# An MM-DiT attention block on one core: fewer changes of the TensorE tiling, text keys in four row groups, and the image gate weights moved ahead of the text V weights

## The chip, the core and the metric

The kernel runs on one core of a Trainium2 chip. The metric is the device time of one execution in microseconds (us); 8 runs of the kernel before have a median of 120.23 us, with 119.77 as the lowest and 120.82 as the highest. The tensor engine is called PE here and its weight loads PEld, the vector engine DVE, the scalar engine ACT, GpSimd POOL, and the sync engine, which only issues DMAs in this kernel, SP.

## What is computed

Two streams of tokens, image (2 batches of 256) and text (2 batches of 32), each of width D = 1152, go through one joint attention. All tensors are bf16.

```python
mod_i = (_silu(c) @ wmod_img).reshape(B, 6, 1, D)      # the same for text: mod_t
shi, sci, gai = mod_i[:, 0], mod_i[:, 1], mod_i[:, 2]  # shift, scale, gate
hi = _layernorm(x_img) * (1 + sci) + shi
qkvi = hi @ wqkv_img                                   # the same for text: qkvt
...
q = jnp.concatenate([qt, qi], axis=1)                  # k and v alike
scores = jnp.einsum('bqd,bkd->bqk', q, k) * D ** (-0.5)
p = _softmax(scores, axis=-1)
a = jnp.einsum('bqk,bkd->bqd', p, v)
at, ai = a[:, :Nt], a[:, Nt:]
out_i = x_img + gai * (ai @ wo_img)
out_t = x_txt + gat * (at @ wo_txt)
```

Of each modulation matrix only three of the six blocks of 1152 columns are used, so 14 weight blocks of 1152 x 1152 (2592 KB each) are read from memory.

## The kernel before

**Weights and their slots.** A block is held as a tile `t` of 128 partitions x 9 x 1152 in one of five slots `w0` to `w4`. SP issues the loads in the order in which they are written at the top of the kernel, and each waits for the readers of the block that held its slot. After the early loads the order is: image shift (slot 2), image Q (3), text shift (0), image K (4), text scale (1), text Q (2), text K (3), text V (1), image gate (0), text gate (2), image output (3), text output (1). So text V waits until text scale has been used on PE, and image gate waits until DVE has read the text shift weights for the last time.

**Order on PE.** The matmuls are pinned to program order (`mm` on line 61, `tr` for transposes on line 64), so PE runs exactly the written sequence: image modulation and V, then `qk_img` for Q and for K (9 groups of 9 matmuls of 512 columns each), then text Q and K (`qk_txt`), scores, text V, attention, output. Between the groups of `qk_img` hooks run small pieces of the text path: `txt_ln`, the text shift on DVE (`txt_shift_part`, accumulator `acc_sh`), `txt_transposes`, then in the K pass `txt_shift_split` (tile `hl`) and `txt_rows_scale` at group 1, `txt_rows_shift`, `txt_cols_shift` and `txt_modulate` at group 6, and `qk_txt(0)` at group 8.

**Tiling of the array.** Most matmuls use the whole 128 x 128 array. Products with few rows in the output are packed side by side in column groups: the modulation products (`mod_rows_of`, `mod_rows`, `vec_rows`) and the text scores use four groups of 32 columns (128*32 in the profile), text V and the text output two of 64 (128*64). The text keys of the attention use two row groups of 64 (64*128). The text transposes of `txt_transposes` have 64 input rows, and those of the text probabilities in `p_transposes` have 32.

**Scores and attention.** The sequence at the end of the projections is `scores_txt`, `scores_img(0)`, `img_gate`, `scores_img(1)`, `v_txt`, `p_transposes(0)`, `txt_gate`, then three `attn_pair` calls with `p_transposes(1)` after the first. Each tile of scores goes through `softmax_tile`: maximum on DVE, exponential on ACT, reciprocal and two or three multiplications on DVE into a tile `pb`. `p_transposes(b)` turns those of one batch into `pT`. The softmax output puts the 32 text keys of batch b at rows 32b of the third key block and again at 64 + 32b; the rows of the other batch are zero, from a memset of `pb` on POOL. `v_txt` likewise leaves the text values twice in `v_t`, at rows 0 and 64.

An attention tile `aps` (128 features x 288 queries of one batch) is a sum over two blocks of image keys and one of text keys. `attn_pair` has three tiles `t0` and three tiles `t1`: image keys for `t0`, then the text keys of all six tiles, then image keys for `t1`. Before, `t0` and `t1` hold six tiles in the order of batch 0, then batch 1. PSUM has six buffers for matmul results (`ps_mm`) and two for transposes (`ps_tr`).

Of the kernel before, what the change touches and what calls it, by code (L numbers as in the profile page):

```python
# [14 lines left out]
def kernel(  # L15
# [14 lines left out]
    nc = tc.nc  # L30
    bf = mybir.dt.bfloat16
# [3 lines left out]
    B, NI, D = x_img.shape  # L35
    NT = x_txt.shape[1]
    P = 128
    KT = D // P
    NTOK = NI + NT
    NIT = (B * NI) // P  # L40
    TPB = NI // P
    NTT = B * NT
# [8 lines left out]
    act = ctx.enter_context(tc.tile_pool(name="act", bufs=1))  # L51
    const = ctx.enter_context(tc.tile_pool(name="const", bufs=1))
# [3 lines left out]
    ps_tr = ctx.enter_context(tc.tile_pool(name="ps_tr", bufs=2, space=PSUM))  # L56
# [3 lines left out]
    def mm(*a, **k):  # L60
        return pin(nc.tensor.matmul(*a, **k))  # L61

    def tr(*a, **k):
        return pin(nc.tensor.transpose(*a, **k))  # L64
# [9 lines left out]
    x_t = act.tile([NTT, D], bf)  # L74
# [9 lines left out]
    def load_w(slot, src, c0, splits=(D,)):  # L84
        t = wtile(slot)
        sv = wview(src, c0)
        o = 0
        for n in splits:
            nc.sync.dma_start(t[:, :, o:o + n], sv[:, :, o:o + n])
            o += n  # L90
        return t
# [22 lines left out]
    w_k_i = load_w(4, wqkv_img, D)  # L114
    w_sc_t = load_w(1, wmod_txt, D)
    w_q_t = load_w(2, wqkv_txt, 0)
    w_k_t = load_w(3, wqkv_txt, D)
    w_v_t = load_w(1, wqkv_txt, 2 * D)
    w_ga_i = load_w(0, wmod_img, 2 * D)
    w_ga_t = load_w(2, wmod_txt, 2 * D)  # L120
    w_o_i = load_rows(3, wo_img, 0)
    w_o_t = load_rows(1, wo_txt, 0)
# [10 lines left out]
    ident = const.tile([P, P], bf)  # L133
# [14 lines left out]
        nc.gpsimd.memset(pick[:, b, b:b + 1], 1.0)  # L148
    shT32 = const.tile([P, KT, 32], bf)
    nc.gpsimd.memset(shT32[:], 0.0)  # L150

    e18 = small.tile([B * KT, P], f32, bufs=1)
    pin(nc.scalar.activation(e18[:], c18[:], ACT.Exp, scale=-1.0))
# [43 lines left out]
    def ln_rstd(var, np_, sign=1.0):  # L197
        rstd = small.tile([P, 1], f32, tag="rstd")
        pin(nc.scalar.activation(rstd[0:np_, :], var, ACT.Ln, bias=eps_t[0:np_], scale=sign))
        pin(nc.scalar.activation(rstd[0:np_, :], rstd[0:np_, :], ACT.Exp, scale=-0.5))  # L200
        return rstd

    def ln_norm(x_ap, mean, rstd, np_, out_ap):
        pin(nc.vector.tensor_scalar(out_ap, x_ap, mean, rstd[0:np_, :], op0=ALU.subtract, op1=ALU.mult))
# [120 lines left out]
    for kt in range(KT):  # L325
        for b in range(B):
            h = hT_i[:, kt, b * NI:(b + 1) * NI]
# [22 lines left out]
    def qk_img(wq, blk, hooks):  # L350
        for j in range(KT):
            for hook in hooks.get(j, ()):
                hook()
            ps = ps_mm.tile([P, B * NI], f32, tag="mm")
            for kt in range(KT):
                mm(ps[:], lhsT=wq[:, kt, j * P:(j + 1) * P], rhs=hT_i[:, kt, :],
                   start=(kt == 0), stop=(kt == KT - 1))
            qk_evac(qkT[:, blk * KT + j, :, 0:NI], ps[:].rearrange("p (b n) -> p b n", b=B), blk)
# [6 lines left out]
    v_t = act.tile([P, D], bf)  # L365
# [5 lines left out]
        nc.scalar.copy(svr[:], p_sv[:])  # L371
        cols["v"] = mod_cols_of(p_sv, "svc")

    xn_t = act.tile([NTT, D], bf)
    xT_t = act.tile([P, KT, NTT], bf)
    hT_t = act.tile([P, KT, NTT], bf)
    mod_t = const.tile([P, 2, KT, B], f32)

    def txt_ln():
        mv = ln_stats(x_t[:, :], NTT)  # L380
        ln_norm(x_t[:, :], mv[0:NTT, 0:1], ln_rstd(mv[0:NTT, 1:2], NTT), NTT, xn_t[:, :])

    def txt_transposes():
        tpt = ps_tr.tile([P, KT, NTT], bf, tag="tr")
        for kt in range(KT):
            tr(tpt[:, kt, :], xn_t[:, kt * P:(kt + 1) * P], ident[0:NTT, 0:NTT])
        nc.scalar.copy(xT_t[:], tpt[:])

    def vec_part(eng, w, acc, r0, r1, bs):
        for kt in range(r0, r1):  # L390
# [101 lines left out]
    def txt_gate():  # L492
        mod_rows(w_ga_t, 1)
        for g in range(2):
            pin(nc.gpsimd.dma_start(xf[64 * g:64 * g + NTT, :, :],
                                    xt_flat.rearrange("t (r g j) -> g t r j", r=2, g=2)[g]))
            for b in range(B):
                r0 = 64 * g + 32 * b
                nc.gpsimd.dma_start(gbf[r0:r0 + NT, :, :],
                                    gsc[1, b, :].rearrange("(r g j) -> g r j", r=2, g=2)[g].partition_broadcast(NT))  # L500
# [2 lines left out]
    shift_v_rows()  # L503
    qk_img(w_q_i, 0, {1: (txt_ln,), 2: (txt_shift_part(0, 3),), 5: (txt_shift_part(3, 6),),
                      6: (txt_transposes,), 8: (txt_shift_part(6, KT),)})
    qk_img(w_k_i, 1, {1: (txt_shift_split, txt_rows_scale,),
                      6: (txt_rows_shift, txt_cols_shift, txt_modulate),
                      8: (lambda: qk_txt(0, w_q_t),)})
    qk_txt(1, w_k_t)

# [1 line left out]
    qpos = [[0, P, 2 * P], [NT, NT + P, 0]]  # L512

    pbs = {}
    PBW = 3 * P
    pb_tiles = [act.tile([P, PBW], bf, name="pb%d" % i) for i in range(2 * B + 1)]
    for t in pb_tiles:
        nc.gpsimd.memset(t[:, NI:PBW], 0.0)

    def softmax_tile(sps, qn, key, parts):  # L520
        nmx = small.tile([P, 1], f32, tag="nmx")
        nc.vector.reduce_max(nmx[0:qn, :], sps[0:qn, :], axis=AX.X, negate=True)
        e = work.tile([P, NTOK], f32, tag="e")
        rs = small.tile([P, 1], f32, tag="rs")
        nc.scalar.activation(e[0:qn, :], sps[0:qn, :], ACT.Exp, bias=nmx[0:qn, :], scale=1.0,
                             accum_out=rs[0:qn, :])
        nc.vector.reciprocal(rs[0:qn, :], rs[0:qn, :])
        pb = pb_tiles[len(pbs)]
        nc.vector.tensor_scalar_mul(pb[0:qn, 0:NI], e[0:qn, 0:NI], rs[0:qn, :])
        for r0, r1, b in parts:  # L530
            nc.vector.tensor_scalar_mul(pb[r0:r1, NI:PBW].rearrange("p (h b n) -> p b h n", h=2, b=B)[:, b],
                                        e[r0:r1, NI:NTOK].unsqueeze(1).to_broadcast([r1 - r0, 2, NT]), rs[r0:r1, :])
        pbs[key] = pb

    def scores_img(b):
        for qi in range(TPB):
            q0 = qi * P
            sps = ps_mm.tile([P, NTOK], f32, tag="mm")
            for ft in range(KT):
                mm(sps[:], lhsT=qkT[:, ft, b, q0:q0 + P], rhs=qkT[:, KT + ft, b, :],  # L540
                   start=(ft == 0), stop=(ft == KT - 1))
            softmax_tile(sps, P, (b, qi), [(0, P, b)])

    def scores_txt():
        sps = ps_mm.tile([P, NTOK], f32, tag="mm")
        for ft in range(KT):
            for b in range(B):
                r0 = 64 * (ft % 2) + NT * b
                mm(sps[r0:r0 + NT, :], lhsT=qkT[:, ft, b, NI:NTOK], rhs=qkT[:, KT + ft, b, :],
                   start=(ft < 2), stop=(ft >= KT - 2), tile_position=(0, r0))  # L550
        half = work.tile([NTT, NTOK], f32, tag="half", bufs=1)
        nc.scalar.copy(half[:], sps[NTT:P, :])  # L552
        nc.vector.tensor_add(half[:], sps[0:NTT, :], half[:])  # L553
        softmax_tile(half, NTT, "t", [(NT * b, NT * (b + 1), b) for b in range(B)])

    pTs = {}

    def p_transposes(b):
        pT_ps = ps_tr.tile([P, 3, NTOK], bf, tag="tr")
        for qi in range(TPB):  # L560
            qp = qpos[b][qi]
            pb = pbs[(b, qi)]
            for kj in range(3):
                tr(pT_ps[:, kj, qp:qp + P], pb[:, kj * P:(kj + 1) * P], ident[:])
        qp = qpos[b][2]
        pb = pbs["t"]
        r0 = NT * b
        for kj in range(3):
            tr(pT_ps[:, kj, qp:qp + NT], pb[r0:r0 + NT, kj * P:(kj + 1) * P], ident[r0:r0 + NT, r0:r0 + NT])
        pT = work.tile([P, 3, NTOK], bf, tag="pT")  # L570
        if b == 0:
            nc.vector.tensor_copy(pT[:], pT_ps[:])
        else:
            nc.scalar.copy(pT[:], pT_ps[:])
        pTs[b] = pT

    def attn_keys(tiles, first):
# [14 lines left out]
    def attn_pair(ids0, ids1):  # L592
        t0 = {key: ps_mm.tile([P, NTOK], f32, tag="mm", name="aps") for key in ids0}
        attn_keys(t0, True)
        t1 = {key: ps_mm.tile([P, NTOK], f32, tag="mm", name="aps") for key in ids1}
        for n, key in enumerate([x for pair in zip(t0, t1) for x in pair]):
            first = key in t1
            r0, (b, dt) = 64 * (n % 2), key
            mm((t1 if first else t0)[key][:], lhsT=v_t[r0:r0 + 64, dt * P:(dt + 1) * P],
               rhs=pTs[b][r0:r0 + 64, 2, :], start=first, stop=not first, tile_position=(r0, 0))  # L600
        attn_evac(t0)
        attn_keys(t1, False)
        attn_evac(t1)

    scores_txt()
    scores_img(0)
    img_gate()
    scores_img(1)
    v_txt()
    p_transposes(0)  # L610
    txt_gate()
    G = [[(b, dt) for dt in range(d0, d0 + 3)] for b in range(B) for d0 in range(0, KT, 3)]
    attn_pair(G[0], G[1])
    p_transposes(1)
    attn_pair(G[2], G[3])
    attn_pair(G[4], G[5])

    def out_img(i, chunks, parts=None):
        b = i // TPB
# [68 lines left out]
```

## Time and profile before

| what | value |
|---|---|
| median of 8 runs | 120.23 us |
| the profiled execution: its time | 120.34 us |
| the profiled execution: its span | 118.5 us |
| PE busy | 112.9 us (95%) |
| DVE busy | 75.4 us (64%) |
| ACT busy | 41.8 us (35%) |
| POOL busy | 10.3 us (9%) |
| clock granted to PE | 1.00 |
| DMA | 40.86 MB, 345 GB/s in the mean, about 410 GB/s from 9 us to 95 us |

The span runs from the first to the last instruction of the profiled execution; its time has 1.84 us more, which lies around it. Times inside the profile count from the start of the span. The profile gives each group of instructions a start, a length and, where an engine was idle before it, the wait. The end of a matmul is modelled, so the length of a stage on PE is read from its start to the start of the next one.

### The profile page before, as it was taken

Reading aid. Unit: us, or ns where it says so; the run is one execution under the profiler, and the core shown is the slowest. Engines: PE = TensorE matmul, PEld = TensorE weight load, DVE = VectorE, ACT = ScalarE, POOL = GpSimd, SP = SyncE. Lnnn points to the kernel's source line nnn. Section 1 sums busy time; section 2 is a strip of 40 time slices with the busy share of each in tenths; the row PEclk is TensorE's granted clock in tenths of the full one; section 3 lists DMA queues with packets and bytes.
Section 4 is the critical chain, followed back from the end, with each engine's and each line's share of the span. In section 5 each row is a group of like instructions: output and inputs, shape, how many; then the busy total and the mean of one; then the engine's idle time right before and its main releaser. Section 6 shows DMA issues by size and latency. Waiting matters only on the chain.

```text
span 118.5 us, 2515 instructions
## 1 busy us (share of the span) xinstructions
PE 112.9 (95%) x1051; PEld 64.3 (54%) x1059; DVE 75.4 (64%) x157; ACT 41.8 (35%) x86; POOL 10.3 (9%) x31
## 2 busy tenths in 40 slices
PE   4998999999999999999999999999999999999990
PEld 1245544445674444445444457877876666656660
DVE  2588492062966799999999540048685666666571
ACT  5799520041752524332029232345327620000000
POOL 7120000000000000000000000000409026000000
PEclk9999999999999999999999999999999999999999
DMA  3999999999999999999999999999999997220223
GB/s 112 370 369 400 408 412 404 413 411 411 411 386 390 413 412 415 401 412 412 411 411 411 415 404 411 413 406 411 404 409 411 410 387 253 109 92 13 100 50 100
DMA packets 18613, 40.86 MB, mean 345 GB/s; under 512 B 1019, under 2 KB 1547, under 8 KB 18603
## 3 DMA queue, kind: packets, MB, share of 16 engines
q1 hardware_dynamic: 17728, 39.56, 86.0%
q0 software_dynamic: 480, 0.89, 2.3%
q10 hardware_dynamic: 395, 0.26, 0.7%
q8 instruction: 8, 0.13, 0.4%
q14 instruction: 2, 0.02, 0.0%
HBM read 39.38 MB, written 1.34 MB: 344 GB/s over the span
## 4 chain that ended last, share of the span: by engine, by line
PE 86%; DMA 8%; DVE 2%; SPq 1%; issue 1%; DVEq 0%
PE ps L61 52%; PE vps L61 15%; DMA t<-in_wmod_img_dram 8%; PE gps L61 6%; PE aps L61 6%; PE sps L61 5%; PE pT_ps L64 1%; PE sc_ps L61 1%; SPq L104 1%; DVE tmp L629 1%; DVE o L630 0%; DVE scc L217 0%; SPq L108 0%; PE tpt L64 0%; PE tp L64 0%
## 5 line engine op out<-in xcount | busy, mean ns | idle before, releaser
L61 PE MATMUL ps<-xT_i,t 128*128 128x512 bf16 x157 | 35.6, 379 | 0.3
L61 PEld LDWEIGHTS <-t 128*128 128x128 bf16 x324 | 20.4, 98 | 19.2 <-issue 0.7
L395 DVE SCALAR_TENSOR_TENSOR acc_sh<-t,sTf,acc_sh 128x1152 f32<-128x1152 bf16 x16 | 21.3, 1400 | 0.0
L61 PE MATMUL ps<-t,aT 128*128 128x384 bf16 (+3 forms) x153 | 20.2, 308 | 0.0
L61 PE MATMUL vps<-t,hS_i 128*128 128x512 bf16 (+1 forms) x106 | 17.8, 325 | 0.2
L61 PEld LDWEIGHTS <-aT 128*128 128x128 bf16 (+1 forms) x153 | 13.0, 101 | 7.1 <-issue 0.5
L61 PEld LDWEIGHTS <-hS_i 128*128 128x128 bf16 x108 | 9.0, 98 | 8.7 <-DVE hS_i L248 0.2
L629 DVE TENSOR_TENSOR tmp<-ps,gb 128x384 bf16<-128x384 f32 (+2 forms) x13 | 6.8, 527 | 6.3 <-PE ps L61 6.3
L346 ACT ACTIVATE qkT<-ps 128x512 bf16<-128x512 f32 (+2 forms) x11 | 6.2, 561 | 12.0 <-PE ps L61 12.0
L61 PE MATMUL wps<-warm 128*128 128x512 bf16 x25 | 8.6, 500 | 1.6 <-DVE unit L132 1.5
L481 POOL DMA_DIRECT2D mod_scratch<-g_sb x4 | 2.5, 636 | 76.4 <-ACT g_sb L174 76.4
L348 ACT CAST qkT<-ps 128x512 bf16<-128x512 f32 (+2 forms) x11 | 5.9, 554 | 8.2 <-PE ps L61 8.2
L172 DVE CAST v_i<-vps 128x512 bf16<-128x512 f32 x5 | 3.5, 692 | 8.2 <-PE vps L61 8.2
L553 DVE TENSOR_TENSOR half<-sps,half 64x288 f32<-64x288 f32 x1 | 0.4, 449 | 9.0 <-ACT half L552 9.0
L587 DVE TENSOR_SCALAR aT<-aps,svc 128x288 bf16<-128x288 f32 x9 | 4.5, 517 | 2.6 <-PE aps L61 2.5
L61 PEld LDWEIGHTS <-warm 128*128 128x128 bf16 x26 | 2.8, 118 | 5.8 <-issue 3.3
L61 PEld LDWEIGHTS <-sT 128*32 128x32 bf16 x180 | 4.4, 96 | 2.6 <-issue 1.8
L174 ACT CAST v_i<-vps 128x512 bf16<-128x512 f32 x4 | 2.3, 580 | 9.9 <-PE vps L61 9.9
L61 PE MATMUL sps<-qkT 128*128 128x288 bf16 (+1 forms) x54 | 5.6, 288 | 0.0
L61 PE MATMUL aps<-pT,v_i 128*128 128x288 bf16 x36 | 5.3, 287 | 0.0
L589 ACT ACTIVATE aT<-aps,svc 128x288 bf16<-128x288 f32 x9 | 4.1, 498 | 3.0 <-PE aps L61 2.9
L61 PE MATMUL gps<-t,sT 128*32 128x288 bf16 x144 | 5.1, 287 | 0.0
(104 smaller groups left out, 108.1 us busy)
## 6 DMA issues: line engine op xcount, KB each, us to landing
t<-in_wqkv_txt_dram SPq DMA_DIRECT2D x3, 2592.0 KB, 17.2
t<-in_wmod_img_dram SPq DMA_DIRECT2D x2, 2592.0 KB, 15.0
t<-in_wqkv_img_dram SPq DMA_DIRECT2D x2, 2592.0 KB, 20.4
t<-in_wmod_txt_dram SPq DMA_DIRECT2D x2, 2592.0 KB, 16.2
t<-in_wmod_txt_dram SPq DMA_DIRECT2D x3, 864.0 KB, 14.2
t<-in_wo_img_dram SPq DMA_DIRECT2D x3, 864.0 KB, 13.0
t<-in_wo_txt_dram SPq DMA_DIRECT2D x3, 864.0 KB, 12.2
t<-in_wqkv_img_dram SPq DMA_DIRECT2D x3, 576.0 KB, 10.1
```

Source lines behind the costliest of these rows:

```text
L61: return pin(nc.tensor.matmul(*a, **k))
L64: return pin(nc.tensor.transpose(*a, **k))
L104: nc.sync.dma_start(x_i[:, b * TPB:(b + 1) * TPB, :], x_img[b].rearrange("(p t) d -> p t d", t=TPB))
L172: nc.vector.tensor_copy(out_ap, in_ap)
L174: nc.scalar.copy(out_ap, in_ap)
L346: nc.scalar.mul(out_ap, in_ap, SCALE)
L348: nc.scalar.copy(out_ap, in_ap)
L395: pin(eng.scalar_tensor_tensor(acc[:, b, :], w[:, kt, :], sTf[:, kt, b:b + 1], acc[:, b, :], op0=ALU.mult, op1=ALU.add))
L481: nc.gpsimd.dma_start(gsc[si, b, :].rearrange("(g j) -> g j", g=NGG), g_sb[b:P:32, :])
L587: nc.vector.tensor_scalar(dst, tiles[(b, dt)][:], bias, None, op0=ALU.add)
L589: nc.scalar.activation(dst, tiles[(b, dt)][:], ACT.Identity, bias=bias)
L629: nc.vector.tensor_mul(tmp[:, 0:n], ps[:, 0:n], gb[:, b, c0:c0 + n])
```

## The change

- Order of loads: the image gate block is loaded before the text V block.
- `txt_ln` writes the normalized text in two halves, features 0 to 639 in rows 0 to 63 and features 640 to 1151 in rows 64 to 127; `txt_transposes` then makes five transposes of 128 x 128 in place of nine of 64 x 128, and two evictions in place of one.
- `txt_rows_scale` moves from group 1 to group 6 of the K pass, directly ahead of `txt_rows_shift`.
- `scores_img(0)` runs ahead of `scores_txt`, so that the text scores and the image gate, which have the same tiling, are neighbours.
- `p_transposes` transposes the text probabilities as whole 128 x 128 tiles. The columns written too much are overwritten by the next transpose. For batch 1 a rotated identity `ident2` brings its rows 32 to 63 to the front. `p_transposes(1)` moves from after the first `attn_pair` to directly after `p_transposes(0)`, ahead of `txt_gate`.
- An `attn_pair` now holds three tiles of batch 0 and the same three of batch 1, and its text keys use four row groups of 32 rows (rows 0, 32, 64, 96).
- The memsets of the `pb` tiles move to the start of POOL's program, together with the new memsets and the two copies that make `ident2`.

```diff
     w_k_t = load_w(3, wqkv_txt, D)
+    w_ga_i = load_w(0, wmod_img, 2 * D)
     w_v_t = load_w(1, wqkv_txt, 2 * D)
-    w_ga_i = load_w(0, wmod_img, 2 * D)
     w_ga_t = load_w(2, wmod_txt, 2 * D)
...
+    KH = (KT + 1) // 2
+    xn_t = act.tile([P, KH * P], bf)
+    nc.gpsimd.memset(pb_txt[:], 0.0)
+    nc.gpsimd.memset(xn_t[NTT:P, (KT - KH) * P:KH * P], 0.0)
+    for t in pb_tiles:
+        nc.gpsimd.memset(t[:, NI:PBW], 0.0)
+    ident2 = const.tile([P, P], bf)
+    nc.gpsimd.tensor_copy(ident2[:, 0:P - NT], ident[:, NT:P])
+    nc.gpsimd.tensor_copy(ident2[:, P - NT:P], ident[:, 0:NT])
...
-        ln_norm(x_t[:, :], mv[0:NTT, 0:1], ln_rstd(mv[0:NTT, 1:2], NTT), NTT, xn_t[:, :])
+        rstd = ln_rstd(mv[0:NTT, 1:2], NTT)
+        for h, (c0, c1) in enumerate(((0, KH * P), (KH * P, D))):
+            ln_norm(x_t[:, c0:c1], mv[0:NTT, 0:1], rstd, NTT, xn_t[NTT * h:NTT * (h + 1), 0:c1 - c0])
...
-        tpt = ps_tr.tile([P, KT, NTT], bf, tag="tr")
-        for kt in range(KT):
-            tr(tpt[:, kt, :], xn_t[:, kt * P:(kt + 1) * P], ident[0:NTT, 0:NTT])
-        nc.scalar.copy(xT_t[:], tpt[:])
+        tpt = ps_tr.tile([P, KH, 2, NTT], bf, tag="tr")
+        for k in range(KH):
+            tr(tpt[:, k].rearrange("p h t -> p (h t)"), xn_t[:, k * P:(k + 1) * P], ident[:])
+        for h, (k0, k1) in enumerate(((0, KH), (KH, KT))):
+            nc.scalar.copy(xT_t[:, k0:k1, :], tpt[:, 0:k1 - k0, h, :])
...
-    qk_img(w_k_i, 1, {1: (txt_shift_split, txt_rows_scale,),
-                      6: (txt_rows_shift, txt_cols_shift, txt_modulate),
+    qk_img(w_k_i, 1, {1: (txt_shift_split,),
+                      6: (txt_rows_scale, txt_rows_shift, txt_cols_shift, txt_modulate),
                       8: (lambda: qk_txt(0, w_q_t),)})
...
-        pT_ps = ps_tr.tile([P, 3, NTOK], bf, tag="tr")
-        for qi in range(TPB):
...
-            tr(pT_ps[:, kj, qp:qp + NT], pb[r0:r0 + NT, kj * P:(kj + 1) * P], ident[r0:r0 + NT, r0:r0 + NT])
+        pT_ps = ps_tr.tile([P, 8 * P], bf, tag="tr")
+
+        def one(kj, pb, qp, perm):
+            o = kj * NTOK + qp
+            tr(pT_ps[:, o:o + P], pb[:, kj * P:(kj + 1) * P], perm[:])
+
+        for kj in range(3):
+            if b:
+                one(kj, pbs["t"], qpos[b][2], ident2)
+            for qi in range(TPB):
+                one(kj, pbs[(b, qi)], qpos[b][qi], ident)
+            if not b:
+                one(kj, pbs["t"], qpos[b][2], ident)
...
-            r0, (b, dt) = 64 * (n % 2), key
-            mm((t1 if first else t0)[key][:], lhsT=v_t[r0:r0 + 64, dt * P:(dt + 1) * P],
-               rhs=pTs[b][r0:r0 + 64, 2, :], start=first, stop=not first, tile_position=(r0, 0))
+            first, (b, dt) = key in t1, key
+            r0 = 64 * (n // 2 % 2) + NT * b
+            mm((t1 if first else t0)[key][:], lhsT=v_t[r0:r0 + NT, dt * P:(dt + 1) * P],
+               rhs=pTs[b][r0:r0 + NT, 2, :], start=first, stop=not first, tile_position=(r0, 0))
...
+    scores_img(0)
     scores_txt()
-    scores_img(0)
     img_gate()
     scores_img(1)
     v_txt()
     p_transposes(0)
+    p_transposes(1)
     txt_gate()
-    G = [[(b, dt) for dt in range(d0, d0 + 3)] for b in range(B) for d0 in range(0, KT, 3)]
-    attn_pair(G[0], G[1])
-    p_transposes(1)
-    attn_pair(G[2], G[3])
-    attn_pair(G[4], G[5])
+    for d0 in range(0, KT, 3):
+        attn_pair(*[[(b, dt) for dt in range(d0, d0 + 3)] for b in range(B)])
```

More of the change, by code (lines that the diff above doesn't have):

```diff
@@ L150 @@
     nc.gpsimd.memset(shT32[:], 0.0)
+    PBW = 3 * P
+    pb_tiles = [act.tile([P, PBW], bf, name="pb%d" % i) for i in range(2 * B)]
+    pb_txt = act.tile([P, PBW], bf, name="pbt")
+    KH = (KT + 1) // 2
[7 more added lines that the diff above has]
+    nc.gpsimd.tensor_copy(ident2[:, P - NT:P], ident[:, 0:NT])
     e18 = small.tile([B * KT, P], f32, bufs=1)
@@ L372, in shift_v_rows @@
         cols["v"] = mod_cols_of(p_sv, "svc")
-    xn_t = act.tile([NTT, D], bf)
     xT_t = act.tile([P, KT, NTT], bf)
@@ L514 @@
     pbs = {}
[L515 to L518, printed above, removed]
     def softmax_tile(sps, qn, key, parts):
@@ L527, in softmax_tile @@
         nc.vector.reciprocal(rs[0:qn, :], rs[0:qn, :])
-        pb = pb_tiles[len(pbs)]
+        pb = pb_txt if key == "t" else pb_tiles[key[0] * TPB + key[1]]
         nc.vector.tensor_scalar_mul(pb[0:qn, 0:NI], e[0:qn, 0:NI], rs[0:qn, :])
@@ L558, in p_transposes @@
     def p_transposes(b):
-        pT_ps = ps_tr.tile([P, 3, NTOK], bf, tag="tr")
-        for qi in range(TPB):
[L561 to L567, printed above, removed]
-        for kj in range(3):
-            tr(pT_ps[:, kj, qp:qp + NT], pb[r0:r0 + NT, kj * P:(kj + 1) * P], ident[r0:r0 + NT, r0:r0 + NT])
+        pT_ps = ps_tr.tile([P, 8 * P], bf, tag="tr")
+        def one(kj, pb, qp, perm):
+            o = kj * NTOK + qp
+            tr(pT_ps[:, o:o + P], pb[:, kj * P:(kj + 1) * P], perm[:])
+        for kj in range(3):
+            if b:
[4 more added lines that the diff above has]
+                one(kj, pbs["t"], qpos[b][2], ident)
+        pT_v = pT_ps[:, 0:3 * NTOK].rearrange("p (k n) -> p k n", k=3)
         pT = work.tile([P, 3, NTOK], bf, tag="pT")
         if b == 0:
-            nc.vector.tensor_copy(pT[:], pT_ps[:])
+            nc.vector.tensor_copy(pT[:], pT_v)
         else:
-            nc.scalar.copy(pT[:], pT_ps[:])
+            nc.scalar.copy(pT[:], pT_v)
         pTs[b] = pT
@@ L596, in attn_pair @@
         for n, key in enumerate([x for pair in zip(t0, t1) for x in pair]):
-            first = key in t1
-            r0, (b, dt) = 64 * (n % 2), key
-            mm((t1 if first else t0)[key][:], lhsT=v_t[r0:r0 + 64, dt * P:(dt + 1) * P],
-               rhs=pTs[b][r0:r0 + 64, 2, :], start=first, stop=not first, tile_position=(r0, 0))
+            first, (b, dt) = key in t1, key
+            r0 = 64 * (n // 2 % 2) + NT * b
+            mm((t1 if first else t0)[key][:], lhsT=v_t[r0:r0 + NT, dt * P:(dt + 1) * P],
+               rhs=pTs[b][r0:r0 + NT, 2, :], start=first, stop=not first, tile_position=(r0, 0))
         attn_evac(t0)
```

## The prediction

> **What bounds the kernel now.** I read the page first, then PE's timeline of the second half, then the issues of the DMA queue and their landings. The page:
>
> ```profile
> PE 112.9 (95%) x1051; PEld 64.3 (54%) x1059; DVE 75.4 (64%) x157; ACT 41.8 (35%) x86; POOL 10.3 (9%) x31
> PE   4998999999999999999999999999999999999990
> DMA  3999999999999999999999999999999997220223
> PE ps L61 52%; PE vps L61 15%; DMA t<-in_wmod_img_dram 8%; PE gps L61 6%; PE aps L61 6%; PE sps L61 5%; PE pT_ps L64 1%; PE sc_ps L61 1%; SPq L104 1%; DVE tmp L629 1%; DVE o L630 0%; DVE scc L217 0%; SPq L108 0%; PE tpt L64 0%; PE tp L64 0%
> ```
>
> PE is in the chain of waits for 86% of the span, without a hole from 14.65 us to the last evictions at 114.8, at clock 1.00. So time taken out of PE's sequence comes off the end one for one, unless something else is late next. The DMA row names the candidate: it is full until 95 us, and weights don't come earlier because PE is earlier. The stages that change, in PE's timeline (start, length, tile of the array, columns, count):
>
> ```profile
> 46.60 0.43 PE L64 MATMUL tpt<-ident,xn_t 64*128 64x64 bf16 x9
> 46.97 7.94 PE L61 MATMUL ps<-xT_i,t 128*128 128x512 bf16 x35
> 54.84 1.29 PE L61 MATMUL gps<-t,sT 128*32 128x288 bf16 x36
> 56.06 9.89 PE L61 MATMUL ps<-xT_i,t 128*128 128x512 bf16 x44
> 65.88 0.67 PE L61 MATMUL gps<-hl,pick 128*32 128x288 bf16 x16
> ...
> 77.14 3.21 PE L61 MATMUL sps<-qkT 128*32 128x288 bf16 x36
> 80.28 1.29 PE L61 MATMUL gps<-t,sT 128*32 128x288 bf16 x36
> 81.50 2.38 PE L61 MATMUL sps<-qkT 128*128 128x288 bf16 x18
> ...
> 86.38 0.68 PE L64 MATMUL pT_ps<-ident,pb 128*128 128x128 bf16 x9
> 86.99 1.29 PE L61 MATMUL gps<-t,sT 128*32 128x288 bf16 x36
> 88.21 0.91 PE L61 MATMUL aps<-pT,v_i 128*128 128x288 bf16 x6
> 89.05 0.54 PE L61 MATMUL aps<-pT,v_t 64*128 64x288 bf16 x6
> 89.52 0.91 PE L61 MATMUL aps<-pT,v_i 128*128 128x288 bf16 x6
> 90.27 0.67 PE L64 MATMUL pT_ps<-ident,pb 128*128 128x128 bf16 x9
> 90.87 0.91 PE L61 MATMUL aps<-pT,v_i 128*128 128x288 bf16 x6
> 91.71 0.72 PE L61 MATMUL aps<-pT,v_t 64*128 64x288 bf16 x6
> 92.36 1.64 PE L61 MATMUL aps<-pT,v_i 128*128 128x288 bf16 x12
> ```
>
> A stage lasts from its start to the next start. See that the text keys of the middle pair take 0.65 us (91.71 to 92.36), the others 0.47.
>
> **Price of a change of tiling.** Single instructions of the trace give it. Matmuls of 512 columns start 216 ns apart; from the last of them to the first of the 36 gate products it is 309 ns. Groups of four of these start 113 ns apart; from the last one back to 512 columns it is 218 ns. So one change costs about 0.10 us (0.093 in, 0.105 out).
>
> **What the Trainium skill says.** "TensorEngine Tiling (Array Packing)", Key Properties: changing the tiling mode, not merely the tile, drains TensorE; the 0.10 us agrees. "TensorE: Matmul & The Clock Gate", Part 3: matmuls in distinct row groups start within about 4 ns of each other and run together, and four tiles of K=32 measured 3.07 times; before, pairs in two row groups start 4 ns apart and the next pair 119 to 130 ns later, but four row groups are in no row of this trace. "DMA: Bandwidth & Descriptors", Queues, rings and completion order: each DMA engine consumes a ring in order; this agrees with loads that land in the order of issue, the 16 pieces of one spread over 2.5 us.
>
> **The change, part by part.**
>
> 1. Text transposes. Before, from the regular end of the 512-column matmul (46.29 + 0.22 = 46.51) to 46.97: 0.46 us, two changes included. After, five transposes of 128 columns at 56 ns (the spacing of `pT_ps` at 86.38), no change of tiling: 0.29. **-0.17.** The norm on DVE becomes two instructions for one of 0.57; I take +0.1 us on DVE, bounds 0 and 0.4. ACT's second copy is hidden: `xT_t` is ready 20 us before its use.
> 2. `txt_rows_scale` beside `txt_rows_shift`: 36 products move, one change in and one out vanish. **-0.20.** The 16 shift products then end at 66.1 (66.48 less 0.37), so DVE's transposes and modulation, which end 3.0 us later, keep their distance of 0.9 to `qk_txt` (70.38, now 70.0). They start at 65.5, their last four at 65.9, and need `hl`, which DVE ends at 65.41; ACT now runs both `hl` copies in succession, which saves about 0.15 and pays for the norm. No wait.
> 3. `scores_img(0)` ahead of `scores_txt`. Before, four changes lie between `qk_txt` and `scores_img(1)`; two vanish (0.20). Within the text scores one group starts 211 ns after its predecessor where the rest take 112: it waits for the last eviction of `qkT` (ACT, 77.25 + 0.32). After, the image scores reach that part 0.7 us after they begin. **-0.30.** Image scores begin at 76.7, text scores at 79.0, gate at 79.6, `scores_img(1)` at 80.8, text V at 83.1.
> 4. `p_transposes`: before, 86.38 to 86.99 and 90.27 to 90.87, 1.21 in all. After, 18 transposes at 55.5 ns, 0.01 at entry and 0.10 at the exit: 1.11. **-0.10.**
> 5. Text keys in four row groups: six matmuls as four and two, so two steps of 119 ns and not three: 0.47 becomes 0.36, thrice 0.12. In the middle pair a wait of 0.18 vanishes as well (it started beside ACT's copy of `pT` of batch 1, 90.97 + 0.88; now that copy, worked out at 87.2 to 88.05 behind the evictions of `v_t`, is 0.8 ahead of its first use at 88.9). **-0.53.**
>
> Sum **-1.30 us**. Output then starts at 93.85 in place of 95.16. Evictions of an `attn_pair`, three each on ACT and DVE in 1.5 us, fit its cycle of 1.93. The last pair now evicts batch 0 features that the first output needs, by 94.1; their turn on PE is at 94.8.
>
> **What is late next.** Softmax: DVE's built order puts the text tile between the two batches. Rebuilt with the lengths of this trace (maximum 0.44, exponential to reciprocal 0.62, multiplications 0.35 and 0.25, text chain 3.4 from half copy to last multiplication) the last probabilities of batch 1 are done at 85.9; before:
>
> ```profile
> 85.86 0.25 DVE L531 TENSOR_SCALAR pb<-e,rs 128x64 bf16<-128x64 f32 x1
> ```
>
> PE now wants them at 86.3, not at 90.3 as before: 0.4 us of slack. Weights: a block takes 6.5 us of the stream. Text K lands at 66.9 (earliest pieces 64.4), then 73.4, 79.9 (now image gate, used at 80.28), then text gate, issued at 72.94:
>
> ```profile
> t<-in_wmod_txt_dram SPq DMA_DIRECT2D x1, 2592.0 KB, 13.3
> ```
>
> So it lands at 86.25, where PE wants it at 86.8 (before 86.99): 0.55 us of slack. The swap matters: with the image gate block at 79.9 and PE there at 79.6, PE would wait 0.3; now it is in place at 73.4, and text V at 79.9 is wanted at 83.1. Moved past SP's queue: the image gate waits for DVE's last read of the text shift weights at 62.6 (plus 0.1), and text V behind it for the scale products, 66.0, not 56.2. At 62.7 only text K is queued, and its first engines run dry at 64.4; the first x load, issued at 0.73 into an empty queue, landed its 576 KB by 4.3, of which transfer is about 1.5, so data flow some 2 us after issue: no gap worth a count, bounds 0 and 1.5 us. Image output weights land by 92.8, wanted from 93.85, its last third at 94.8. POOL's additions (two memsets, two copies, and the `pb` memsets, 0.79 before, moved ahead; about 1.7 us) lie in its idle 2.66 us before 5.48, and `sel` follows later; if they overran, the modulation products at 10.2 still have 4 us. The gate row on POOL starts 1.3 earlier with image gate, so its broadcast does too.
>
> The profiled execution took 120.34 us, 118.5 of span and 1.84 around it; less 1.30 it is 119.04. The median of the runs is 0.11 below it: **118.9 us**.
>
> **Rivals.**
>
> A. A wait takes the place of what is removed: probabilities or text gate weights come 0.6 to 1.3 us later than worked out. For: slacks of 0.4 and 0.55 against a sum from one execution. Against: both ends come from measured lengths. Each microsecond past the slack costs one: 119.1 to 119.8.
>
> B. Four row groups don't overlap. If only two run together, step 5 keeps 0.18: 119.3. If none do, six steps of 119 ns make 0.83 a pair, +0.36 twice and +0.18, sum +0.13 for the change: 120.4. Against: column groups of 32 do overlap in fours (113 ns a group), and pairs of row groups do.
>
> C. Slower: the weight stream runs dry at 64 to 67 us, since image gate now is issued behind text K alone and nothing is queued behind it until 66. Every later block slips by the gap. Decisive point: beyond 0.55 us the text gate at 86.8 waits one for one; the gain is gone at 1.85 and it is slower by over 0.3% from 2.2. With a gap of 3 us: 120.23 - 1.30 + 2.45 = 121.4. Against: 4.2 us lie between issue and text K's end.
>
> D. The change doesn't do what it says: the built order shows five and 18 whole transposes, both moves and the swap, so I give it nothing.
>
> **Chances.** As worked out (118.5 to 119.3): 0.76. A: 0.10. B: 0.08, half of it within 0.3% of before. C: 0.06. About 0.3% (0.36 us) is what a measurement of this kernel can tell from no change. Faster 0.88, same 0.06, slower 0.06. The range of 118.3 to 119.9 takes in A and the nearer part of B; C and the far end of B are left out.
>
> **What would show it.** Right: `tpt` x5 without a gap, 36 and 16 `gps` products adjacent, image scores starting at 76.7, 18 transposes in 1.1 us from 85.7, text keys in 0.36, output from 93.85. Wrong: PE idle before the text gate, released by DMA (C, A) or before a transpose, released by DVE (A); six text key starts 119 ns apart (B); DMA share below 9 tenths between 62 and 70 us (C).

## The result and the profile after

The changed kernel takes 118.91 us in the median, the kernel before 120.25 us in the same comparison: a ratio of 0.9888, with a 95% interval of 0.9863 to 0.9912. Slow executions at a lower granted clock are left out of every median and ratio here: one of the changed kernel (194.93 us at 0.572), and three with the old order of loads (123.72 to 124.40 us at 0.971 to 0.986). The profiled execution took 119.09 us, with a span of 117.3 us.

The page after, for the lines of the page shown of before (engines, PE's row, the rate of the DMA in GB/s, the chain of waits by engine and by line):

```profile
PE 111.0 (95%) x1047; PEld 64.0 (55%) x1055; DVE 75.5 (64%) x158; ACT 41.8 (36%) x87; POOL 11.2 (10%) x34
...
PE   4997999999999999999999999999999999999990
...
GB/s 104 386 394 401 399 410 407 411 411 413 413 396 366 409 412 411 407 410 412 411 414 384 337 406 409 414 405 410 405 411 408 410 381 413 190 99 7 101 50 101
...
PE 55%; DVE 24%; DMA 14%; issue 3%; SPq 1%; ACT 1%; DVEq 0%; ACTq 0%
PE ps L61 28%; DVE acc_sh L409 16%; PE vps L61 12%; DMA t<-in_wmod_img_dram 8%; DMA x_t<-in_x_txt_dram 6%; PE aps L61 5%; PE sps L61 4%; PE gps L61 3%; DVE hl L417 2%; DVE acc_sh L407 1%; DVE stats L194 1%; PE pT_ps L64 1%; PE sc_ps L61 1%; SPq L104 1%; DVE tmp L640 1%
```

PE is still full in nearly every slice and has lost 1.9 us of busy time. The chain has changed: 24% of it now runs over DVE, through `acc_sh` and `hl`, and 6% over the load of `x_t`. In the kernel before, no part of that path was in the chain. The DMA rate has a dip that it did not have, 384 and 337 in slices 21 and 22 (of 40, counted from 0), about 62 to 67 us. The row of the kernel before, which has 411 and 415 there:

```profile
GB/s 112 370 369 400 408 412 404 413 411 411 411 386 390 413 412 415 401 412 412 411 411 411 415 404 411 413 406 411 404 409 411 410 387 253 109 92 13 100 50 100
```

PE's timeline of the stages that changed (start, length, tile of the array, columns, count):

```profile
46.37 0.44 PE L64 MATMUL tpt<-ident,xn_t 128*128 128x128 bf16 x5
46.65 17.65 PE L61 MATMUL ps<-xT_i,t 128*128 128x512 bf16 x79
64.23 1.29 PE L61 MATMUL gps<-t,sT 128*32 128x288 bf16 x36
65.34 0.98 PE L61 MATMUL gps<-hl,pick 128*32 128x288 bf16 x16
66.25 4.06 PE L61 MATMUL ps<-xT_i,t 128*128 128x512 bf16 x17
...
76.82 3.09 PE L61 MATMUL sps<-qkT 128*128 128x288 bf16 x36
79.62 1.39 PE L61 MATMUL gps<-t,sT 128*32 128x288 bf16 x36
80.94 2.38 PE L61 MATMUL sps<-qkT 128*128 128x288 bf16 x18
...
86.39 0.28 PE L64 MATMUL pT_ps<-ident,pb 128*128 128x128 bf16 x2
...
86.72 0.28 PE L64 MATMUL pT_ps<-ident,pb 128*128 128x128 bf16 x2
86.93 1.29 PE L61 MATMUL gps<-t,sT 128*32 128x288 bf16 x36
...
88.99 0.42 PE L61 MATMUL aps<-pT,v_t 32*128 32x288 bf16 x6
89.34 1.64 PE L61 MATMUL aps<-pT,v_i 128*128 128x288 bf16 x12
...
93.94 20.17 PE L61 MATMUL ps<-t,aT 128*128 128x384 bf16 x153
```

Three things are to be seen. The text keys (`v_t`) take 0.35 us from their start to the next start, where they took 0.47 and once 0.65. The output starts at 93.94, 1.22 us earlier than before. And the 16 shift products, 65.34 to 66.25, take 0.91 us where they took 0.60 and should now take no more: single matmuls show that the last four start 418 ns after the third group, not 113. They wait for DVE:

```profile
63.30 2.66 DVE L417 TENSOR_TENSOR hl<-acc_sh,hl 128x1152 bf16<-128x1152 f32 x2
```

`hl` is ready at 65.96 and the last four products start at 66.01.

**A measure finer than the time.** One execution differs from the next mainly in when its first image V matmul starts (13.83 to 15.33 us in the profiles of this study), because that waits for the first modulation weights. From there to the first output matmul PE's sequence repeats to about 0.01 us, waits apart. I call this the stretch. Before, it is 80.51 us (14.65 to 95.16); in the profile after, 79.42 us, of which 0.31 is the wait for `hl`. What follows the stretch on PE takes 20.2 us in both kernels.

### The profile page after: what moved, and what is told of

Read it like the earlier page. It is cut to its first block, busy times and chain, and to the rows that moved or that the text cites. A ratio compares the mean times of both kernels' runs of the same rounds, so it can differ in the third digit from the quotient of the medians.

```text
span 117.3 us, 2511 instructions
## 1 busy us (share of the span) xinstructions
PE 111.0 (95%) x1047; PEld 64.0 (55%) x1055; DVE 75.5 (64%) x158; ACT 41.8 (36%) x87; POOL 11.2 (10%) x34
## 4 chain that ended last, share of the span: by engine, by line
PE 55%; DVE 24%; DMA 14%; issue 3%; SPq 1%; ACT 1%; DVEq 0%; ACTq 0%
PE ps L61 28%; DVE acc_sh L409 16%; PE vps L61 12%; DMA t<-in_wmod_img_dram 8%; DMA x_t<-in_x_txt_dram 6%; PE aps L61 5%; PE sps L61 4%; PE gps L61 3%; DVE hl L417 2%; DVE acc_sh L407 1%; DVE stats L194 1%; PE pT_ps L64 1%; PE sc_ps L61 1%; SPq L104 1%; DVE tmp L640 1%
## 5 line engine op out<-in xcount | busy, mean ns | idle before, releaser
L61 PE MATMUL ps<-t,aT 128*128 128x384 bf16 (+3 forms) x153 | 20.2, 308 | 0.0
L61 PE MATMUL wps<-warm 128*128 128x512 bf16 x25 | 7.7, 458 | 1.7 <-DVE unit L132 1.5
L532 DVE TENSOR_REDUCE nmx<-sps 128x1 f32<-128x288 f32 x4 | 1.7, 451 | 8.9 <-PE sps L61 8.9
L61 PE MATMUL ps<-hT_t,t 128*128 128x64 bf16 x162 | 5.0, 193 | 0.0
```

## Experiments

Two theories stood against each other at the start. The first: PE's sequence sets the time, each part gains what it takes out of it, and a new wait for `hl` costs 0.3 us in the changed kernel. The second: the waits that the change uncovers, of DVE or of the weights, take the place of what was removed, and a part that looks cheap holds up another.

**The control** is the changed kernel itself, unedited.

> The changed kernel itself, as a control beside its variants. Both theories: about 118.9 us. The theory that the new wait for hl on DVE belongs to the kernel expects the gap in the last four shift products of the text (tile gps from hl and pick) again, 0.2 to 0.4 us long; the rival that it was a chance of one execution expects none, with PE 0.3 us earlier from there on.

Measured: 118.94 us. Its profiled execution has no gap in the shift products:

```profile
64.66 0.66 PE L61 MATMUL gps<-hl,pick 128*32 128x288 bf16 x16
65.25 1.04 PE L61 MATMUL ps<-xT_i,t 128*128 128x512 bf16 x3
```

The stretch is 79.11 us, 0.31 shorter than in the first profile. `hl` was ready 51.06 us after the first image V matmul; PE wanted it at 51.20, and in the first profile it came at 51.45. The difference is the load of `x_t`: DVE began its statistics 22.45 us after that matmul here and 22.83 there. So the wait is not part of every execution, and the first theory's systematic 0.3 us falls. Two more profiles with the same norm and the same late issue of `x_t`, of the old order of loads and of the row groups undone below, have no wait either (`hl` at 50.90 and 50.96). What remains is that the slack is about 0.1 us.

**The load of `x_t` earlier**, on ACT's queue:

```diff
+    pin(nc.scalar.dma_start(x_t[:], xt_flat[:, :]))
     v_open(A1, 0, 3)
...
-    pin(nc.scalar.dma_start(x_t[:], xt_flat[:, :]))
     v_open([(3, 1)], 0, KT)
```

> The changed kernel with the load of x_t issued on ACT's queue some 15 us earlier, so that the text norm on DVE need not wait for it. Theory: in the changed kernel the chain x_t load, norm, acc_sh, hl ends 0.3 us after PE wants hl; with x_t there in time DVE starts its statistics at about 35.8 instead of 37.3, hl is ready about 1.5 us earlier, the gap of 0.3 in the text shift products goes, and the image gate block is issued 1.5 us earlier, so the dip of the DMA rate at 62 to 67 us goes too. Time 0.3 us below the control. Rival: the 0.3 is taken back at the text gate, whose weights land at 86.5 where PE then comes at 86.6, or the earlier x_t delays the V weights at 15 to 20 us: same time as the control, within 0.1, with a wait released by DMA.

Measured: 118.93 us, and a stretch of 79.11. DVE starts its statistics 21.15 us after the first image V matmul and `hl` is ready at 49.72, 1.5 us before it is wanted. The time does not move, so the wait for `hl` is not worth anything that the median shows; with six and seven runs an effect of 0.3 us could hide there, and what speaks is the equal stretch. The DMA rate in slices 21 and 22 is 411 and 410: the dip of the first profile is gone as well. The control had only a trace of it, 415 and 394, and it cost PE nothing there.

**The text norm delayed**: its two instructions issued twice, alone and with the earlier `x_t`.

```diff
-        for h, (c0, c1) in enumerate(((0, KH * P), (KH * P, D))):
+        for h, (c0, c1) in 2 * tuple(enumerate(((0, KH * P), (KH * P, D)))):
```

> The changed kernel with the two instructions of the text norm issued twice, so that DVE is 0.85 us later with acc_sh and hl. Theory: the changed kernel has only about 0.1 us of slack between hl and the last text shift products (before: 0.8), so PE waits 0.7 to 0.8 there, the stretch from the first image V matmul to the first output matmul goes from 79.11 to about 79.9, and the median to about 119.6. Image gate is issued 0.85 later too; the weight stream's gap grows to about 2 us and may add up to 0.5 at the text gate. Rival: DVE has slack, the one wait of 0.3 was a late x_t alone: below 0.2 of difference.

> The same with the norm issued twice, and the load of x_t issued some 15 us earlier. Theory: the early load gives DVE about 1.3 us more slack, which covers the 0.85: no wait at the text shift products, a stretch of 79.11, a median of about 118.9. Rival: what is lost by the doubled norm is lost through the later image gate load or the load of x_t is not what holds DVE's chain: a stretch of 79.3 or more.

Measured: alone 119.84 us (ratio to before 0.9992, interval 0.9967 to 1.0017, where the control has 0.9907), with a stretch of 80.20, 1.10 longer. PE's timeline shows where:

```profile
64.75 0.54 PE L61 MATMUL gps<-hl,pick 128*32 128x288 bf16 x12
66.20 0.31 PE L61 MATMUL gps<-hl,pick 128*32 128x288 bf16 x4 [0.91 <-DVE hl L417]
```

The last four products start 1.20 us after the third group, 1.09 more than without a wait. `hl` came 1.17 us later than in the control (52.23 against 51.06 after the first image V matmul), so the slack there was 0.08 us. The expectation had 0.7 to 0.8: the second norm lengthened the chain by 0.93 and not by 0.85, and that `hl` itself took 0.2 longer was not counted. With the earlier `x_t` the same doubled norm costs nothing: 119.06 us and a stretch of 79.11. This shows the chain: load of `x_t`, norm, `acc_sh`, `hl`, shift products.

**The old text norm and transposes** in the changed kernel:

```diff
...
-        for h, (c0, c1) in enumerate(((0, KH * P), (KH * P, D))):
-            ln_norm(x_t[:, c0:c1], mv[0:NTT, 0:1], rstd, NTT, xn_t[NTT * h:NTT * (h + 1), 0:c1 - c0])
+        ln_norm(x_t[:, :], mv[0:NTT, 0:1], ln_rstd(mv[0:NTT, 1:2], NTT), NTT, xn_t[:, :])
...
-        for k in range(KH):
-            tr(tpt[:, k].rearrange("p h t -> p (h t)"), xn_t[:, k * P:(k + 1) * P], ident[:])
+        for kt in range(KT):
+            tr(tpt[:, kt, :], xn_t[:, kt * P:(kt + 1) * P], ident[0:NTT, 0:NTT])
...
```

> The changed kernel with the old text norm (one instruction) and the old nine text transposes of 64 rows. Theory: PE pays 0.17 more at the text transposes, but DVE's norm takes 0.41 less (0.49 in place of 0.90), so hl is ready 0.4 earlier against a PE that is 0.17 later, the 0.30 wait goes, and the time is 0.1 us below the control. Rival, the prediction's own step 1: the five whole transposes gain what they save on PE, so without them the time is 0.17 above the control.

Measured: 118.72 us (ratio to before 0.9878, interval 0.9849 to 0.9907; the control has 0.9907, 0.9871 to 0.9942). The median is 0.2 below the control's, which would speak against the new transposes, but the intervals overlap over more than half of the narrower one, so the time does not decide. The stretch does for PE: 79.30 us, 0.19 longer than the control's. `hl` was ready 50.97 us after the first image V matmul although `x_t` was as late as in the first profile (22.77), and PE did not wait. So the new transposes are worth 0.19 us when `x_t` comes in time; in the first profile, where it came late, the wait after their slower norm took 0.31 back.

**The old order of loads** in the changed kernel:

```diff
-    w_ga_i = load_w(0, wmod_img, 2 * D)
     w_v_t = load_w(1, wqkv_txt, 2 * D)
+    w_ga_i = load_w(0, wmod_img, 2 * D)
```

> The changed kernel with the two loads in the old order, text V ahead of image gate. Theory: text V now is issued at 65.6 (it waits for the text scale products), image gate behind it; the stream delivers text V at about 74 and image gate at about 80.3, where PE wants it at 79.6. PE waits 0.5 to 1.0 us at the image gate, released by DMA, and the time is that much above the control. Rival: the swap is without effect, since the sum of bytes is the same and the text gate is the tight load either way: within 0.1 of the control.

Measured: 122.44 us over three runs (121.57, 122.44 and 123.18), ratio to before 1.0181 (1.0123 to 1.024), slower than the kernel before. PE's timeline, and the DMA rate of the page:

```profile
83.09 1.29 PE L61 MATMUL gps<-t,sT 128*32 128x288 bf16 x36 [2.87 <-DMA t<-in_wmod_img_dram]
```

```profile
GB/s 115 377 365 392 400 413 403 412 413 413 410 383 391 413 410 414 402 412 413 410 413 210 170 409 406 417 400 411 414 400 413 414 386 403 172 57 46 98 49 98
```

The image gate starts at 83.09 where it would have started at 79.94, and the stretch is 82.16 us, 3.05 longer than the control's and three times the most that was expected. Slices 21 and 22 are at 210 and 170 GB/s. Against 411 that is 442 GB/s missing for a slice of 3.0 us, 1.3 MB, or 3.2 us of the stream. Text V, which waits for the moved scale products, was issued at 66.19. The pieces of text K, the last load in the queue, had landed from 64.48 to 66.71, so that one DMA engine after the other had nothing to do, and image gate stood behind text V in the queue. This is the prediction's rival C, in the place where the swap prevents it. The control's 118.94 and these 3.05 make 121.99; the three runs, 1.6 us apart, lie around that and leave no remainder that could be read.

**One part alone, on the kernel before: row groups.** Batches paired, four row groups, batch 1's transposes moved ahead of the gate but in their old form:

```diff
-            r0, (b, dt) = 64 * (n % 2), key
+            r0 = 64 * (n // 2 % 2) + NT * b
...
     p_transposes(0)
+    p_transposes(1)
     txt_gate()
...
```

> The kernel before with one part of the change: attention pairs of both batches, text keys in four row groups of 32, and batch 1's probability transposes ahead of the text gate; the transposes keep their old form. Theory (step 5 of the prediction): three times 0.12 for the text keys and 0.18 for the wait in the middle pair, so the stretch on PE from the first image V matmul to the first output matmul is 0.53 us shorter than before (80.51), at 79.98; the median is 0.5 below before. Rival (B): four row groups run only two at a time, the text keys stay at 0.47 a pair and only the 0.18 is saved: 80.33.

Measured: 119.66 us, ratio 0.9966 (0.9946 to 0.9987), stretch 79.96, 0.55 shorter. PE's timeline:

```profile
89.25 0.42 PE L61 MATMUL aps<-pT,v_t 32*128 32x288 bf16 x6
89.60 1.64 PE L61 MATMUL aps<-pT,v_i 128*128 128x288 bf16 x12
91.17 0.42 PE L61 MATMUL aps<-pT,v_t 32*128 32x288 bf16 x6
91.52 1.64 PE L61 MATMUL aps<-pT,v_i 128*128 128x288 bf16 x12
```

Each set of text keys takes 0.35 us, also that of the middle pair. The four row groups start 3 to 4 ns apart and the next two 123 ns later. Rival B falls.

**The row groups undone** in the changed kernel (two groups of 64, the rest kept):

```diff
-            r0 = 64 * (n // 2 % 2) + NT * b
-            mm(..., lhsT=v_t[r0:r0 + NT, ...], rhs=pTs[b][r0:r0 + NT, 2, :], ...)
+            r0 = 64 * (n % 2)
+            mm(..., lhsT=v_t[r0:r0 + 64, ...], rhs=pTs[b][r0:r0 + 64, 2, :], ...)
```

> The changed kernel with the text keys of its attention pairs back in two row groups of 64, all else kept. Theory: each of the three pairs takes 0.47 for its text keys in place of 0.35, so the stretch from the first image V matmul to the first output matmul is 0.36 longer than the changed kernel's (79.1 where it does not wait for hl), at 79.47, and the median about 0.3 above 118.9. Rival: the pairing of the batches and the early transposes make the gain of step 5, the row groups none of it: no difference to the changed kernel.

Measured: 119.27 us, ratio 0.9916 (0.9889 to 0.9943), which the time alone does not tell from the control's; stretch 79.48, 0.37 longer than the control's. Step 5's two terms are both there: 0.37 from the row groups, and 0.18, what is left of the 0.55 of the run before, from the wait.

**The scale products and the swap alone**, on the kernel before (both hunks of the change, nothing else):

> The kernel before with two parts of the change: the text scale products moved beside the text shift products, and the image gate load ahead of text V. Theory (step 2): 0.20 to 0.23 us less on PE: 80.28 from the first image V matmul to the first output matmul. hl is ready in time since the text norm is still one instruction. Rival: PE reaches the last shift products before hl is ready and waits, as in the profiled execution of the changed kernel (0.3): 80.4 to 80.6, no gain.

Measured: 119.92 us, ratio 0.9974 (0.995 to 0.9998), stretch 80.28, 0.22 shorter. No wait for `hl`: it is ready 50.53 us after the first image V matmul, where the control has 51.06. Of the difference 0.41 is the norm, which is one instruction here; in the rest, `x_t` came 0.13 earlier.

**The order of scores alone**, on the kernel before:

```diff
-    scores_txt()
     scores_img(0)
+    scores_txt()
```

> The kernel before with one part of the change: image scores of batch 0 ahead of the text scores. Theory (step 3): two changes of tiling fewer (0.20) and the 0.10 wait for the last eviction of qkT gone, so the stretch from the first image V matmul to the first output matmul is 0.30 to 0.33 us shorter than before: 80.2. Rival: the image gate weights, which land at 79.9 in the old order of loads and are wanted at 79.95 then, hold PE, and up to 0.3 is given back: 80.2 to 80.5 with a wait released by DMA at the gate.

Measured: 120.31 us, ratio 1.0001 (0.998 to 1.0021), stretch 80.68, which is 0.17 longer. PE and DVE in the timeline:

```profile
89.06 0.91 PE L61 MATMUL aps<-pT,v_i 128*128 128x288 bf16 x6 [0.43 <-DVE pT L572]
```

```profile
88.41 0.59 DVE L572 COPY pT<-pT_ps 128x864 bf16<-128x864 bf16 x1
```

The gate of image weights did not wait, so the stated rival is not the cause. PE saved its 0.33 us and then stood 0.50 us ahead of the first attention matmul, which needs DVE's eviction of `pT`. DVE runs that after the last probabilities of batch 1 and two evictions of `v_t`, and with the text tile between the batches its chain ends later.

**Scores and transposes together**: the same with `p_transposes(1)` ahead of the gate, in its old form.

> The kernel before with image scores ahead of text scores, and batch 1's probability transposes, in their old form, ahead of the text gate. Alone, the order of scores gave nothing: PE saved 0.33 us and then waited 0.50 for the softmax chain on DVE, at the first attention matmul. Theory: the 0.6 us of transposes moved ahead of that matmul fill the wait, all but what the transposes themselves wait for the last probabilities (done 72.4 us after the first image V matmul, wanted at 72.2); with the 0.18 of the middle pair the stretch from the first image V matmul to the first output matmul is 80.51 - 0.33 - 0.18 + 0.3 = 80.3. Rival: the wait isn't DVE's and comes again in full: 80.5 or more.

Measured: 119.91 us, ratio 0.9968 (0.9949 to 0.9988), stretch 80.20, 0.31 shorter than before. The wait ahead of the attention is gone; the transposes of batch 1 take 0.81 us in place of 0.61, which is the 0.2 that they wait for probabilities. Of the 0.31, 0.18 is the wait of the middle pair, so the order of scores itself is worth 0.13 here: it gains with the early transposes, but not its whole 0.33 as in the changed kernel.

Two more things differ in the changed kernel, which these two runs do not have. Its transposes of batch 1 are whole and go key block by key block. And its DVE, in the order that was built, takes the two maxima of batch 1 in a row, where these two kernels put the second behind the reciprocal of the first tile. The maxima in the changed kernel's first profile, then the second maximum in the kernel with the order of scores alone, whose reciprocal stands at 85.81:

```profile
83.71 0.82 DVE L532 TENSOR_REDUCE nmx<-sps 128x1 f32<-128x288 f32 x2
```

```profile
85.89 0.44 DVE L522 TENSOR_REDUCE nmx<-sps 128x1 f32<-128x288 f32 x1
```

From the start of `scores_img(1)` to the last probabilities it is 5.28 us in the control and 5.91 in the two kernels here. This 0.63 is more than the 0.50 that PE stood. So whether the order of scores needs the moved transposes, or only DVE's other order, was not separated.

## Why the prediction was right

The forecast was 118.9 us and the median is 118.91. That they agree to 0.01 is chance: the interval of the ratio is about 0.3 us wide to either side. What carries is the sum. Its steps, against the stretch of the control, which has no wait:

| step | predicted | measured |
|---|---|---|
| 1, text transposes | -0.17 | -0.18 in place, -0.19 when undone |
| 2, scale beside shift | -0.20 | -0.23 in place, -0.22 alone |
| 3, order of scores | -0.30 | -0.33 in place; +0.17 alone |
| 4 and 5, transposes and row groups | -0.63 | -0.66 in place; step 5 alone -0.55 |
| sum | -1.30 | -1.40; -1.08 in the first profile with its wait |

Steps 1 to 3 and the joint row are differences of start times between the kernel before and the control, counted from the first image V matmul. Step 4 was not run apart; by difference it is -0.11. The terms are one to three hundredths too small. Part of that is that a change of tiling costs a little more than the 0.093 and 0.105 used: of the gate products the second group of four starts 123 ns after the first, where the later ones start 113 apart. The two waits of rival A did not come: in the control, with the early `x_t` and with the row groups undone the text gate starts 72.10 us after the first image V matmul, and in the first profile 72.42, which is these 72.10 and the wait for `hl`.

Where it was wrong:

- **Step 2, "No wait".** The profiled execution waited 0.31 us. The term behind it was the norm on DVE, "I take +0.1 us on DVE, bounds 0 and 0.4": measured from the start of the norm to the start of `acc_sh` it is 0.90 us against 0.49, so +0.41, just outside the bounds. The hidden slack of 0.5 us that the step showed shrank to about 0.1, and an `x_t` that lands 0.4 us late uses it up.
- **The price of the swap.** The prediction said that PE "would wait 0.3" at the image gate without it. The run showed 3.05 us. It had kept the old landing times, although the move of the scale products makes text V wait until 66 us, and in the old order image gate stands behind text V. A step that was moved was not followed through the queue of the order that it was compared with.
- **"0.4 us of slack" of the softmax chain.** The last probabilities were worked out at 85.9, which is 71.25 us after the first image V matmul. In the control they came at 71.39; in the first profile at 86.23, with PE's wait of 0.31 ahead of them:

```profile
85.71 0.35 DVE L539 TENSOR_SCALAR pb<-e,rs 128x256 bf16<-128x256 f32 x1
85.98 0.25 DVE L541 TENSOR_SCALAR pb<-e,rs 128x64 bf16<-128x64 f32 x1
```

  No wait followed. The second transpose of the pair at 86.39 reads the image keys of this tile, ready at 86.06; its text keys, ready at 86.23, are read only by the second of the pair at 86.72. So some 0.3 us were left, near the 0.4. What the prediction did not see is that on the kernel before the order of scores brings a wait for DVE with it.
- **Rival C** happened in small: image gate was issued at 63.41, and text K had landed at 65.97, its first pieces at 64.32. The rate dipped by 101 GB/s over two slices, 0.3 MB or 0.7 us. The text gate weights landed at 86.50, where PE came at 86.93: the slack of 0.55 became 0.43, and held. But 0.31 of it is PE's own wait for `hl`. In the control 0.33 was left, with the early `x_t` 0.99, and in the profile with the row groups undone, an edit that acts only behind this gate, 0.07 (landed at 86.52, PE at 86.59). So it was in part luck that no profile shows a wait here.

## What to carry to other kernels

Where PE is full, count its changes of tiling and the steps of its tiled groups from start times of single matmuls: such a sum was right to 0.1 us in 1.3. Then ask of every part what it needs covered. Here one reordering gained nothing alone on the old kernel, and one move made the load order decisive, so the parts alone, on the old kernel and taken out of the new, tell more than the total.

## What the runs showed of the hardware that I had not expected

- How late a load may be issued without a gap in the stream shows at image gate, or text V in the old order, behind text K. Issued 2.3 us before the first piece of text K landed (the early `x_t`), it left no gap; 1.9 us before (the control) the stream lost about 0.1 us, 0.9 us before (the first profile) 0.7, and 1.7 us after (the old order of loads) 3.2. The losses are estimates from slices 21 and 22 of the rows of GB/s, against 411.
- PE's sequence from the first image V matmul to the output repeats to 0.01 us between the executions of this study (the start of the text transposes is 31.86 us after that matmul in seven profiles of kernels with the new transposes, 31.96 in six with the old ones), while its start moves by 1.5 us.
- Splitting one DVE instruction of 64 x 1152 (0.57 us) into one of 64 x 640 and one of 64 x 512 that writes to the other 64 partitions cost 0.41 us more on the chain, although the elements are the same in number. The three instructions take 0.57, 0.44 and 0.41 us for 1152, 640 and 512 elements a partition, which lies on one line with about 0.27 us at no elements (an estimate from these three). That speaks for the second instruction as the cost, and not for the other partitions; no run separates the two.
